# A kernel without the 60 unread one-column products in its order of work

## The chip, the cores and the metric

The kernel runs on one core of a Trainium2 chip. The metric is the time of one execution on the device in microseconds (us). A run is an execution of the whole program; the time before is given as the median of three runs.

## The reference

Two parts follow each other. A recurrent attention (RWKV-7) runs over 768 time steps for 4 batches of 8 heads with a 40 x 40 state, and its output, seen as 3072 tokens of 320 numbers, goes through two dense layers with h * cos(h) between them.

```python
# r, k, v, w, a, b: (4, 8, 768, 40)
for t in range(S):
    kt, vt, rt = (k[:, :, t], v[:, :, t], r[:, :, t])
    wt, at, bt = (w[:, :, t], a[:, :, t], b[:, :, t])
    y[:, :, t] = np.einsum('bhd,bhde->bhe', rt, state)
    Sa = np.einsum('bhde,bhe->bhd', state, at)
    state_decay = state * wt[:, :, None, :] - np.einsum('bhd,bhe->bhde', Sa, bt)
    state = state_decay + np.einsum('bhd,bhe->bhde', vt, kt)
x = y.transpose(0, 2, 1, 3).reshape(3072, 320)
h = x @ w_in               # w_in: (320, 2048)
g = h * np.cos(h)
out = g @ w_out            # w_out: (2048, 320)
```

## The kernel before

The 768 steps are cut into 24 chunks of 32 steps. Within a chunk the recurrence is turned into small matrix products over 32 x 32 and 40 x 72 blocks, one for each batch and head, which TensorE (PE) runs in corners of its array; from chunk to chunk only the state is handed on, in the tile qz. The dense layers then take two chunks at a time, a group of 256 tokens (12 groups), with products of 128 rows and 128, 160 or 256 columns.

The order of all work is written out by hand. The string PLAN is a list of some two thousand tokens, and one loop at the end runs the function of each token (table ACTS); nothing reorders them, so each engine's queue holds its instructions in the order of the tokens. A token is a name and its numbers. Those that matter here:

- of the recurrence, with the chunk's number: g (tile gram), t (sT), q (qps), x (x0ps), s (sps), z (dps, and on DVE, the vector engine, qz and yt), k (kT), pn (nps, for two chunks);
- ij, steps of the inverse of a triangular matrix, on DVE (inv, inv_tmp);
- of the dense layers, with the group's and the block's number: fa and fb (the first layer: tile ph, read by the tile turns and the product gT), m and ms (the second layer: po and p);
- P, the function shifted_, which the change concerns.

PE's tiles stand in eight banks: four, used in turn, for the recurrence (pool ps_a, by the helper at), two for ph, two for po. Nearly all products are recorded by one helper, mm, so that they all bear line L210. A product of 32-bit floats runs as two passes on PE, each a weight load (PEld) and a product; a transpose runs as one.

P:60 stands once in the list, in the middle of the dense layers' group 7, between r:22 (which has no work on PE) and fa:7:3. On PE it follows the products po of m:7:2:0 and comes ahead of the products ph of fa:7:3 and the products dps of z:17.

```python
def shifted_(n):
    ps = at("pad")
    for _ in range(n):
        mm(ps[:1, :1], idle[:, :1], idle[:, :1], True)
```

The tile idle is 128 x 128 zeros in bf16, written at the start; the tile pad is a bank of ps_a that nothing reads. Each of the 60 is a weight load of one column and a product of one column.

Of the kernel before, what the change touches and what calls it, by code (L numbers as in the profile page):

```python
# [90 lines left out]
u:7:0:0 u:7:0:1 m:7:0:0 u:7:0:2 u:7:0:3 lt:21:a ld:23:b pt:r:5:2 z:16 r:23 kn:18 m:7:0:1 t:17 q:17 fa:7:2  # L91
o:6:0 st:r:5:2 st:r:5:1 tk:16 fb:7:2 x:17 xa:20 rf:v:5 u:7:1:0 u:7:1:1 m:7:1:0 u:7:1:2 lt:22:a k:18 y:7:2:0
xa:21 s:17 pn:20 m:7:1:1 lt:22:w xw:22 lt:23:a y:7:2:2 lt:19:r y:7:2:1 m:7:2:0 o:6:1 pt:v:5:0 u:7:1:3 r:22
P:60 fa:7:3 z:17 tb:16 fb:7:3 lt:23:w y:7:3:0 u:7:2:0 tk:17 tb:17 u:7:2:1 u:7:2:2 u:7:2:3 y:7:3:1 y:7:3:2 t:18
g:18 m:7:2:1 m:7:3:0 st:v:5:0 ld:19:k xa:22 xw:23 xa:23 u:7:3:0 u:7:3:1 q:18 pb:22 ld:19:v sp:20 u:7:3:2
m:7:3:1 c:7:0 c:7:1 c:7:3 pt:v:5:1 pn:22 fa:8:0 is:20 ij:20:31 ij:20:30 pt:v:5:2 fb:8:0 x:18 y:8:0:0 ij:20:29
kn:19 u:7:3:3 ms:7 y:8:0:1 y:8:0:2 ij:20:28 s:18 c:7:2 ij:20:27 k:19 ij:20:26 st:v:5:1 ld:20:k lt:21:r
ij:20:25 u:8:0:0 ij:20:24 fa:8:1 u:8:0:1 z:18 ld:20:v fb:8:1 lt:19:v g:19 kn:20 t:19 st:v:5:2 m:8:0:0 ij:20:23
u:8:0:2 ld:21:k ij:20:22 ij:20:21 lt:20:v q:19 y:8:1:0 tk:18 y:8:1:2 ld:21:v k:20 m:8:0:1 y:8:1:1 lt:20:r
ij:20:20 x:19 o:7:0 ij:20:19 m:8:1:0 u:8:1:0 u:8:1:1 u:8:1:2 u:8:0:3 u:8:1:3 ij:20:18 ij:20:17 fa:8:2 ij:20:16  # L100
s:19 fb:8:2 tb:18 z:19 y:8:2:1 m:8:1:1 y:8:2:0 y:8:2:2 o:7:1 tk:19 tb:19 t:20 ij:20:15 ij:20:14 fa:8:3
ij:20:13 ij:20:12 ij:20:11 u:8:2:0 u:8:2:1 q:20 kn:21 fb:8:3 g:20 y:8:3:0 y:8:3:1 k:21 m:8:2:0 u:8:2:2 u:8:2:3
y:8:3:2 ij:20:10 ij:20:9 m:8:2:1 ij:20:8 ij:20:7 ij:20:6 ij:20:5 lt:21:v g:21 u:8:3:0 ij:20:4 ij:20:3 fa:9:0
ij:20:2 ij:20:1 ie:20 m:8:3:0 u:8:3:1 u:8:3:2 u:8:3:3 x:20 fb:9:0 y:9:0:1 m:8:3:1 c:8:0 c:8:1 s:20 lt:22:v
ms:8 c:8:2 ld:22:k y:9:0:0 y:9:0:2 c:8:3 fa:9:1 z:20 ld:22:v kn:22 ld:23:v u:9:0:0 m:9:0:0 u:9:0:1 u:9:0:2
tk:20 t:21 q:21 fb:9:1 y:9:1:1 y:9:1:0 lt:22:r u:9:0:3 y:9:1:2 x:21 m:9:0:1 lt:23:r fa:9:2 s:21 tb:20 fb:9:2
y:9:2:0 z:21 u:9:1:0 u:9:1:1 m:9:1:0 u:9:1:2 u:9:1:3 ld:23:k k:22 t:22 g:22 q:22 m:9:1:1 o:8:0 o:8:1 y:9:2:1
y:9:2:2 u:9:2:0 u:9:2:1 fa:9:3 fb:9:3 x:22 tk:21 m:9:2:0 u:9:2:2 u:9:2:3 y:9:3:0 y:9:3:1 y:9:3:2 lt:23:v kn:23
s:22 m:9:2:1 u:9:3:0 z:22 u:9:3:1 tb:21 fa:10:0 fb:10:0 y:10:0:1 y:10:0:0 m:9:3:0 u:9:3:2 t:23 k:23 m:9:3:1
c:9:0 u:9:3:3 ms:9 y:10:0:2 fa:10:1 c:9:1 q:23 c:9:2 c:9:3 u:10:0:0 fb:10:1 u:10:0:1 m:10:0:0 u:10:0:2  # L110
m:10:0:1 tk:22 u:10:0:3 y:10:1:1 y:10:1:0 y:10:1:2 g:23 o:9:0 fa:10:2 u:10:1:0 u:10:1:1 tb:22 m:10:1:0 o:9:1
u:10:1:2 x:23 fb:10:2 y:10:2:0 y:10:2:1 y:10:2:2 s:23 u:10:1:3 m:10:1:1 u:10:2:0 fa:10:3 u:10:2:1 z:23 tk:23
fb:10:3 y:10:3:1 m:10:2:0 u:10:2:2 m:10:2:1 y:10:3:0 y:10:3:2 m:10:3:0 u:10:3:0 u:10:3:1 u:10:3:2 u:10:2:3
u:10:3:3 tb:23 fa:11:0 fb:11:0 y:11:0:1 y:11:0:0 y:11:0:2 m:10:3:1 c:10:0 ms:10 c:10:1 c:10:3 c:10:2 fa:11:1
fb:11:1 u:11:0:0 u:11:0:1 m:11:0:0 u:11:0:2 o:10:0 y:11:1:0 u:11:0:3 y:11:1:1 m:11:0:1 u:11:1:0 y:11:1:2
u:11:1:1 fa:11:2 fb:11:2 m:11:1:0 u:11:1:2 u:11:1:3 y:11:2:1 y:11:2:0 y:11:2:2 m:11:1:1 fa:11:3 u:11:2:0
u:11:2:1 fb:11:3 y:11:3:0 m:11:2:0 u:11:2:2 m:11:2:1 y:11:3:1 u:11:3:0 y:11:3:2 o:10:1 u:11:3:1 m:11:3:0
u:11:2:3 u:11:3:2 m:11:3:1 c:11:0 c:11:1 u:11:3:3 ms:11 c:11:2 o:11:0 c:11:3 o:11:1
"""

GROUPS = "0+1 2+3 4+5 6+7 8+9 10+11 12+13 14+15 16+17 18+19 20+21 22+23"
# [1109 lines left out]
```

## Time and profile before

| | |
|---|---|
| time, median of 3 runs | 762.61 us (758.38 to 766.61) |
| the profiled execution | 755.39 us, span 753.7 us from the first to the last instruction |
| mean granted clock of PE | 0.983 |
| busy: PE, weight loads (PEld), DVE, ACT, POOL | 702.8, 578.2, 534.8, 398.0, 245.8 us |
| tile pad | 60 products on PE from 541.9 to 543.4 us, 163 ns each, overlapping |
| queue 8, kind "instruction" | 141 packets, 2.31 MB |

PE's products are pipelined, so 60 that take 163 ns each can stand within 1.6 us. A row of the timeline gives the start, how long the merged instructions took, engine, line, operation, tile written <- tiles read, shape, how many, and in brackets how long the engine was idle before and what released it; "issue" there means that the profile shows nothing that it waited for. A row of the windows gives a stretch in us, its length, the busy time and number of instructions of PE, PEld, DVE, ACT and POOL, PE's granted clock, the DMA engines' busy share and GB/s. A piece of the chain of waits gives start, duration and what ran. A DMA queue's row gives packets, MB and the share of the 16 DMA engines' time.

### The profile page before, as it was taken

The numbers are of one execution on the slowest core, as the hardware profiler recorded it, in microseconds if no ns is written. First come the engines' busy times: TensorE is split into PE (matmuls) and PEld (weight loads), VectorE is DVE, ScalarE is ACT, GpSimd is POOL, SyncE is SP. The second block draws the span as 40 slices with busy tenths as digits, with TensorE's granted clock in tenths as the row PEclk, the third lists the DMA queues.
The fourth block names the chain that finished last, engine by engine and source line by source line (L and its number), as shares of the span: only waits on it lengthen the run. The fifth ranks groups of instructions, "written<-read, shape, count | busy, mean of one in ns | idle before, by whom it ended". The sixth has DMA issues, their size and how long they took to land.

```text
span 753.7 us, 40220 instructions
## 1 busy us (share of the span) xinstructions
PE 702.8 (93%) x17956; PEld 578.2 (77%) x17956; DVE 534.8 (71%) x1199; ACT 398.0 (53%) x764; POOL 245.8 (33%) x427
## 2 busy tenths in 40 slices
PE   4659899999999999989999999999999999999995
PEld 2546577777777777878888888888888788888885
DVE  7799888976467777568987758998367984534442
ACT  1335575775656665655645746546456444544442
POOL 8545304221241442450440442332242412321211
PEclk9779999999999999999999999999999999999998
DMA  7667455564565657655656667557543212110000
GB/s 118 130 168 183 149 152 136 116 132 75 117 119 113 123 107 145 130 130 115 139 118 110 128 130 155 107 118 120 102 78 76 62 41 59 48 29 13 21 18 17
DMA packets 267580, 78.11 MB, mean 104 GB/s; under 512 B 229104, under 2 KB 260848, under 8 KB 267408
## 3 DMA queue, kind: packets, MB, share of 16 engines
q1 hardware_dynamic: 264976, 73.66, 46.7%
q8 instruction: 141, 2.31, 1.3%
q0 software_dynamic: 1344, 1.72, 1.2%
q10 hardware_dynamic: 1088, 0.16, 0.1%
q14 instruction: 31, 0.25, 0.1%
HBM read 54.53 MB, written 20.97 MB: 100 GB/s over the span
## 4 chain that ended last, share of the span: by engine, by line
PE 69%; DVE 13%; ACT 5%; DMA 4%; SPq 4%; issue 3%; POOL 1%; DVEq 0%; POOLq 0%; ACTq 0%
PE ph L210 28%; PE po L210 17%; PE dps L210 4%; PE x0ps L210 4%; PE gram L210 3%; PE p L210 3%; SPq L262 2%; PE sps L210 2%; PE qps L210 2%; DVE inv L659 2%; PE nps L210 2%; DVE inv_tmp L655 2%; DVE gT L1010 2%; PE sT L807 1%; DMA nat_v<-in_v_dram 1%
## 5 line engine op out<-in xcount | busy, mean ns | idle before, releaser
L210 PE MATMUL ph<-xT,w_in_sb 128*128 128x256 f32 x768 | 184.3, 386 | 2.5 <-issue 1.0
L210 PEld LDWEIGHTS ph<-xT,w_in_sb 128*128 128x128 f32 x768 | 139.8, 190 | 31.1 <-issue 12.0
L210 PE MATMUL po<-w_out_sb,gT 128*128 128x160 f32 (+1 forms) x624 | 130.3, 347 | 3.0 <-DVE gT L1010 2.3
L1002 DVE SCALAR_TENSOR_TENSOR turns<-turns,ph 128x512 f32<-128x512 f32 x96 | 63.6, 685 | 93.5 <-ACT turns L1000 93.2
L1000 ACT ACTIVATE turns<-ph,few 128x512 f32<-128x512 f32 x96 | 63.6, 686 | 120.2 <-PE ph L210 110.1
L210 PEld LDWEIGHTS po<-w_out_sb,gT 128*128 128x128 f32 x624 | 97.1, 190 | 21.5 <-DVE gT L1010 3.3
L917 POOL TENSOR_TENSOR qz<-qz,wc 128x160 f32<-128x160 f32 x92 | 40.0, 457 | 132.5 <-DVE qz L916 132.5
L1010 DVE TENSOR_TENSOR gT<-ph,turns 128x512 f32<-128x512 f32 x96 | 64.4, 684 | 21.1 <-ACT turns L1007 20.8
L1007 ACT ACTIVATE turns<-turns,few 128x512 f32<-128x512 f32 x96 | 69.3, 722 | 3.1
L1006 ACT ACTIVATE turns<-turns 128x512 f32<-128x512 f32 x96 | 60.1, 626 | 12.4 <-DVE turns L1002 12.3
L1090 POOL TENSOR_TENSOR s<-gT 128x256 f32<-128x256 f32 x36 | 26.9, 747 | 97.3 <-DVE gT L1086 97.3
L210 PE MATMUL ph<-xT,w_in_tail 64*128 64x256 f32 (+1 forms) x464 | 54.5, 396 | 0.0
L291 ACT COPY nat_a<-ws 128x416 f32<-128x416 f32 (+1 forms) x45 | 45.1, 1019 | 16.9 <-DMA wdv<-nat_a 5.7
L210 PE MATMUL po<-TW,gT 128*128 128x160 f32 x288 | 51.4, 300 | 1.8 <-DVE gT L1086 1.2
L659 DVE TENSOR_TENSOR inv<-inv,inv_tmp 128x31 f32<-128x31 f32 (+15 forms) x124 | 50.0, 404 | 4.2
L1082 POOL TENSOR_TENSOR s<-gT 128x256 f32<-128x256 f32 x36 | 27.2, 757 | 78.7 <-DVE gT L1010 72.7
L825 ACT COPY qz<-qps 40x256 f32<-40x256 f32 x92 | 33.8, 367 | 30.8 <-PE qps L210 29.3
L655 DVE TENSOR_TENSOR inv_tmp<-u,inv 128x31 f32<-128x31 f32 (+15 forms) x124 | 46.5, 375 | 2.7
L566 POOL TENSOR_TENSOR bn<-nat_b,rw 128x320 f32<-128x320 f32 x22 | 19.3, 878 | 84.8 <-DVE rw L565 39.2
L210 PEld LDWEIGHTS po<-TW,gT 128*128 128x128 f32 x288 | 42.9, 190 | 2.8 <-DVE gT L1086 1.9
L565 DVE RECIPROCAL rw<-nat_w 128x320 f32<-128x320 f32 x20 | 42.6, 2139 | 0.0
L916 DVE TENSOR_TENSOR qz<-dps,qz 128x160 f32<-128x160 f32 x92 | 29.2, 317 | 16.8 <-PE dps L210 16.8
(158 smaller groups left out, 1248.5 us busy)
## 6 DMA issues: line engine op xcount, KB each, us to landing
words<-in_moe_w_in_dram SPq DMA_DIRECT2D x8, 512.0 KB
xd<-yt SPq DMA_DIRECT2D x48, 80.0 KB
out_dram<-ot SPq DMA_DIRECT2D x24, 160.0 KB
nat_v<-in_v_dram SPq DMA_DIRECT2D x90, 40.0 KB
nat_k<-in_k_dram SPq DMA_DIRECT2D x90, 40.0 KB
nat_b<-in_b_dram SPq DMA_DIRECT2D x84, 40.0 KB
wd<-ws SPq DMA_DIRECT2D x5, 640.0 KB
nat_w<-wd SPq DMA_DIRECT2D x80, 40.0 KB
```

Source lines behind the costliest of these rows:

```text
L210: nc.tensor.matmul(o, lhsT=lhsT, rhs=rhs, start=start, stop=stop, skip_group_check=True)
L291: nc.scalar.copy(quad_part(n, q, i).rearrange("p (d t) -> p d t", t=C), ws[:, :, PARTS[i]].rearrange("p t d -> p d t"))
L565: nc.vector.reciprocal(rw, wn)
L655: nc.vector.tensor_tensor(tmp, u[:, j : j + 1, :j].to_broadcast([P, C - j, j]), x[:, j:, j : j + 1].to_broadcast([P, C - j, j]), ALU.mult,)
L659: nc.vector.tensor_tensor(x[:, j:, :j], x[:, j:, :j], tmp, ALU.subtract)
L825: nc.scalar.copy(pick(qz[rows], f * (NZ - C), (NZ, 2 * B), (1, C)), ps[f][rows, : 2 * B * C].rearrange("p (i t) -> p i t", t=C),)
L917: nc.gpsimd.tensor_tensor(z, z, wc.rearrange("p (b f m) -> p f m b" if re_laid("w", c // 4) else "p (f m b) -> p f m b", f=2, m=2)[:, :, : ...
L1000: nc.scalar.activation(t, u, ACTF.Identity, bias=rnd, scale=1.0)
L1002: nc.vector.scalar_tensor_tensor(t, t, -ROUND, u, ALU.add, ALU.subtract)
L1006: nc.scalar.activation(t, t, ACTF.Abs)
L1007: nc.scalar.activation(t, t, ACTF.Sin, bias=half_pi, scale=-2.0 * math.pi)
L1010: nc.vector.tensor_tensor(gT[:, 2 * e : 2 * e + 2, :n], phs[e], ns[e].rearrange("p (f t) -> p f t", f=2), ALU.mult)
```

## The change

The token P:60 is taken out of PLAN. The lines of the string are filled anew, which changes nothing but where they break; the tokens' order stays. The function shifted_ stays, unused.

```diff
 ... m:7:2:0 o:6:1 pt:v:5:0 u:7:1:3 r:22
-P:60 fa:7:3 z:17 tb:16 fb:7:3 lt:23:w y:7:3:0 u:7:2:0 tk:17 tb:17 u:7:2:1 u:7:2:2 u:7:2:3 y:7:3:1 y:7:3:2 t:18
-g:18 m:7:2:1 m:7:3:0 ...
+fa:7:3 z:17 tb:16 fb:7:3 lt:23:w y:7:3:0 u:7:2:0 tk:17 tb:17 u:7:2:1 u:7:2:2 u:7:2:3 y:7:3:1 y:7:3:2 t:18 g:18
+m:7:2:1 m:7:3:0 ...
```

In the program, PE has 60 weight loads and 60 products fewer at that place; the other engines' queues and SP's DMA queue hold the same instructions in the same order.

More of the change, by code (lines that the diff above doesn't have):

```diff
@@ L93 @@
 xa:21 s:17 pn:20 m:7:1:1 lt:22:w xw:22 lt:23:a y:7:2:2 lt:19:r y:7:2:1 m:7:2:0 o:6:1 pt:v:5:0 u:7:1:3 r:22
-P:60 fa:7:3 z:17 tb:16 fb:7:3 lt:23:w y:7:3:0 u:7:2:0 tk:17 tb:17 u:7:2:1 u:7:2:2 u:7:2:3 y:7:3:1 y:7:3:2 t:18
-g:18 m:7:2:1 m:7:3:0 st:v:5:0 ld:19:k xa:22 xw:23 xa:23 u:7:3:0 u:7:3:1 q:18 pb:22 ld:19:v sp:20 u:7:3:2
-m:7:3:1 c:7:0 c:7:1 c:7:3 pt:v:5:1 pn:22 fa:8:0 is:20 ij:20:31 ij:20:30 pt:v:5:2 fb:8:0 x:18 y:8:0:0 ij:20:29
-kn:19 u:7:3:3 ms:7 y:8:0:1 y:8:0:2 ij:20:28 s:18 c:7:2 ij:20:27 k:19 ij:20:26 st:v:5:1 ld:20:k lt:21:r
@@ L98 @@
[L98 to L117, printed above, removed]
@@ L118 @@
-u:11:2:3 u:11:3:2 m:11:3:1 c:11:0 c:11:1 u:11:3:3 ms:11 c:11:2 o:11:0 c:11:3 o:11:1
+fa:7:3 z:17 tb:16 fb:7:3 lt:23:w y:7:3:0 u:7:2:0 tk:17 tb:17 u:7:2:1 u:7:2:2 u:7:2:3 y:7:3:1 y:7:3:2 t:18 g:18
+m:7:2:1 m:7:3:0 st:v:5:0 ld:19:k xa:22 xw:23 xa:23 u:7:3:0 u:7:3:1 q:18 pb:22 ld:19:v sp:20 u:7:3:2 m:7:3:1
+c:7:0 c:7:1 c:7:3 pt:v:5:1 pn:22 fa:8:0 is:20 ij:20:31 ij:20:30 pt:v:5:2 fb:8:0 x:18 y:8:0:0 ij:20:29 kn:19
+u:7:3:3 ms:7 y:8:0:1 y:8:0:2 ij:20:28 s:18 c:7:2 ij:20:27 k:19 ij:20:26 st:v:5:1 ld:20:k lt:21:r ij:20:25
@@ new lines @@
+u:8:0:0 ij:20:24 fa:8:1 u:8:0:1 z:18 ld:20:v fb:8:1 lt:19:v g:19 kn:20 t:19 st:v:5:2 m:8:0:0 ij:20:23 u:8:0:2
+ld:21:k ij:20:22 ij:20:21 lt:20:v q:19 y:8:1:0 tk:18 y:8:1:2 ld:21:v k:20 m:8:0:1 y:8:1:1 lt:20:r ij:20:20
+x:19 o:7:0 ij:20:19 m:8:1:0 u:8:1:0 u:8:1:1 u:8:1:2 u:8:0:3 u:8:1:3 ij:20:18 ij:20:17 fa:8:2 ij:20:16 s:19
+fb:8:2 tb:18 z:19 y:8:2:1 m:8:1:1 y:8:2:0 y:8:2:2 o:7:1 tk:19 tb:19 t:20 ij:20:15 ij:20:14 fa:8:3 ij:20:13
+ij:20:12 ij:20:11 u:8:2:0 u:8:2:1 q:20 kn:21 fb:8:3 g:20 y:8:3:0 y:8:3:1 k:21 m:8:2:0 u:8:2:2 u:8:2:3 y:8:3:2
@@ new lines @@
+ij:20:10 ij:20:9 m:8:2:1 ij:20:8 ij:20:7 ij:20:6 ij:20:5 lt:21:v g:21 u:8:3:0 ij:20:4 ij:20:3 fa:9:0 ij:20:2
+ij:20:1 ie:20 m:8:3:0 u:8:3:1 u:8:3:2 u:8:3:3 x:20 fb:9:0 y:9:0:1 m:8:3:1 c:8:0 c:8:1 s:20 lt:22:v ms:8 c:8:2
+ld:22:k y:9:0:0 y:9:0:2 c:8:3 fa:9:1 z:20 ld:22:v kn:22 ld:23:v u:9:0:0 m:9:0:0 u:9:0:1 u:9:0:2 tk:20 t:21
+q:21 fb:9:1 y:9:1:1 y:9:1:0 lt:22:r u:9:0:3 y:9:1:2 x:21 m:9:0:1 lt:23:r fa:9:2 s:21 tb:20 fb:9:2 y:9:2:0 z:21
+u:9:1:0 u:9:1:1 m:9:1:0 u:9:1:2 u:9:1:3 ld:23:k k:22 t:22 g:22 q:22 m:9:1:1 o:8:0 o:8:1 y:9:2:1 y:9:2:2
@@ new lines @@
+u:9:2:0 u:9:2:1 fa:9:3 fb:9:3 x:22 tk:21 m:9:2:0 u:9:2:2 u:9:2:3 y:9:3:0 y:9:3:1 y:9:3:2 lt:23:v kn:23 s:22
+m:9:2:1 u:9:3:0 z:22 u:9:3:1 tb:21 fa:10:0 fb:10:0 y:10:0:1 y:10:0:0 m:9:3:0 u:9:3:2 t:23 k:23 m:9:3:1 c:9:0
+u:9:3:3 ms:9 y:10:0:2 fa:10:1 c:9:1 q:23 c:9:2 c:9:3 u:10:0:0 fb:10:1 u:10:0:1 m:10:0:0 u:10:0:2 m:10:0:1
+tk:22 u:10:0:3 y:10:1:1 y:10:1:0 y:10:1:2 g:23 o:9:0 fa:10:2 u:10:1:0 u:10:1:1 tb:22 m:10:1:0 o:9:1 u:10:1:2
+x:23 fb:10:2 y:10:2:0 y:10:2:1 y:10:2:2 s:23 u:10:1:3 m:10:1:1 u:10:2:0 fa:10:3 u:10:2:1 z:23 tk:23 fb:10:3
@@ new lines @@
+y:10:3:1 m:10:2:0 u:10:2:2 m:10:2:1 y:10:3:0 y:10:3:2 m:10:3:0 u:10:3:0 u:10:3:1 u:10:3:2 u:10:2:3 u:10:3:3
+tb:23 fa:11:0 fb:11:0 y:11:0:1 y:11:0:0 y:11:0:2 m:10:3:1 c:10:0 ms:10 c:10:1 c:10:3 c:10:2 fa:11:1 fb:11:1
+u:11:0:0 u:11:0:1 m:11:0:0 u:11:0:2 o:10:0 y:11:1:0 u:11:0:3 y:11:1:1 m:11:0:1 u:11:1:0 y:11:1:2 u:11:1:1
+fa:11:2 fb:11:2 m:11:1:0 u:11:1:2 u:11:1:3 y:11:2:1 y:11:2:0 y:11:2:2 m:11:1:1 fa:11:3 u:11:2:0 u:11:2:1
+fb:11:3 y:11:3:0 m:11:2:0 u:11:2:2 m:11:2:1 y:11:3:1 u:11:3:0 y:11:3:2 o:10:1 u:11:3:1 m:11:3:0 u:11:2:3
@@ L119 @@
+u:11:3:2 m:11:3:1 c:11:0 c:11:1 u:11:3:3 ms:11 c:11:2 o:11:0 c:11:3 o:11:1
 """
```

## The prediction

> **What bounds the kernel now.** I read the first part of the page, then the windows by stage, then the chain of waits.
>
> ```profile
> span 753.7 us, 40220 instructions
> PE 702.8 (93%) x17956; PEld 578.2 (77%) x17956; DVE 534.8 (71%) x1199; ACT 398.0 (53%) x764; POOL 245.8 (33%) x427
> ```
> ```profile
> 541.90:600.00 58.10, 57.58 (x1661) 49.70 (x1664) 40.09 (x105) 29.24 (x59) 21.28 (x35) 1.00 0.32 67
> 600.00:650.00 50.00, 49.32 (x1387) 42.47 (x1380) 34.00 (x90) 25.67 (x54) 12.96 (x21) 1.00 0.23 54
> 650.00:700.00 50.00, 49.71 (x1080) 42.47 (x1079) 21.55 (x52) 21.25 (x41) 11.57 (x17) 1.00 0.08 21
> ```
> TensorE (PE, first column of busy time) sets the end: behind the 60 products, from 541.9 to 700 us, it is idle for 1.5 us of 158, and its clock is granted in full (1.00). What is taken from PE there, or put in its way, reaches the end nearly whole. The 60 products stand at 541.9:
>
> ```profile
> 537.88 2.37 PE po L210 x16
> 540.26 0.50 issue
> 540.75 1.25 PE po L210 x8
> 542.00 1.57 PE pad L210 x60
> 543.57 1.92 PE ph L210 x8
> ```
> The chain of waits ran through them: PE goes from po to pad to ph without a pause, so they hide in no wait. The 0.50 us of "issue" just ahead is the other thing to see: PE stands still, and nothing in the profile releases it. The timeline of PE's weight loads shows that stop and some more of them:
>
> ```profile
> 332.88 0.24 PEld L210 LDWEIGHTS gram<-rT,vp 40*32 40x32 f32 x31 [0.96 <-issue]
> ...
> 448.81 0.30 PEld L210 LDWEIGHTS ph<-xT,w_in_sb 128*128 128x128 f32 x2 [1.39 <-issue]
> ...
> 470.94 0.49 PEld L210 LDWEIGHTS gram<-rT,vp 40*32 40x32 f32 x46 [0.44 <-issue]
> ...
> 540.76 0.46 PEld L210 LDWEIGHTS po<-w_out_sb,gT 128*128 128x128 f32 x3 [0.61 <-issue]
> ```
> They fall in the middle of a run of like products, where nothing is waited for. I counted PE's queue in program order (weight loads, products and waits on semaphores; an f32 product is two passes, a load and a product each, a transpose is one): these four stand at places 16578, 22722, 23746 and 27330. Divided by 256, each leaves 194. Between 300 and 541.9 us PE stops for over 0.2 us at nine places with that remainder, 5.5 us in all; behind the 60 products it stops at none. The DMA view of that later stretch says what comes every 256 instructions:
>
> ```profile
> q8 instruction: 32, 0.52, 1.3%
> ```
> This is queue 8 from 541.9 to 700 us: 32 packets of 16 KB, in the time in which the windows count 4128 products and 4123 loads, so one for about 256 instructions. These are PE's own instructions on their way in. Before the stop at 540.76 the packet began at 538.34 and took 0.93 us, and PE went on 1.49 us after its end; the next one began at 541.89, 1.13 us after PE had gone on. So PE holds the block that it is in and the next; when it steps into a block it sends for the one after. From that step to use: 1.05 us until the packet starts (0.8 to 1.2 at 23 of the 34 edges behind the 60 products), 0.95 us for the packet (0.88 to 1.36 there), 1.45 us until PE can use it (1.37 to 1.58 at the nine stops): **3.45 us, an estimate from these rows**. PE stops where it runs 256 instructions in less. On average a block takes 4.9 us, but 128 small gram products are 256 instructions in some 1.3 us. Behind the 60 products as they now stand, the block edges fall so that the shortest block takes 3.43 us (580.40 to 583.83), and it just passes.
>
> **The change, part by part.** Removed: 60 products and 60 weight loads on PE and the tile pad; no row waits for pad. On the other engines and on SP's queue no instruction is added, removed or moved.
>
> (1) The products themselves. From 541.93, the first pad, to 543.50, the first ph, is 1.57 us, on the path. The ph products behind need nothing later than what po had, so all of it goes: **-1.57 us**. Bounds: 0, if PE then waits for something else, and -1.57.
>
> (2) The bank of pad. Four banks go round; pad took one, and the four dps tiles of z:17 follow at once and take all four, with or without it. Nothing is late for it: 0.
>
> (3) All that PE does behind place 27346 stands 120 instructions earlier. In the old count the block edges move by 120, to remainder 314 - 256 = 58. I laid the new edges over the old timeline and asked of each block how long PE takes from entering it to needing the next (PE reads a run of instructions some 8 ahead, as its semaphore instructions show, but not past a wait: 10 places behind the wait for kT that ended at 229.16 it sent for a block at 229.35). Against 3.45 us:
>
> - 608.05 (gram) to 610.11 (ph): 2.06 us, so a stop of **1.4**.
> - 645.9 (gram, just after its wait for kT) to 647.21 (qps): 1.3 us, a stop of **2.1**. This block holds 227 instructions of gram and 29 of qps.
> - 685.30 (po) to 688.12 (x0ps): 2.82 us, a stop of **0.6**; the block ahead of it, entered at 682.0 in gram, is **0.15** late, which takes away the lead that po would have had.
> - 622.2 (ph) to 625.59 (dps), **0.1**; 632.35 (x0ps) to 635.68 (ph), **0.1**; 654.5 (x0ps) to 657.85 (sps) and on to 661.13 (dps), **0.15 each**.
> - 581.1 to 584.63, across po and x0ps: 3.5 us, **0**. PE had read ahead: a semaphore instruction 13 places behind the edge ran at 581.13.
>
> The rest have 0.2 us or more to spare. The rows of the two dearest places:
>
> ```profile
> 608.05 0.76 PE L210 MATMUL gram<-aT,kT 40*32 40x32 f32 x64
> 608.68 0.75 PE L210 MATMUL gram<-rT,vp 40*32 40x32 f32 x64
> 609.36 1.99 PE L210 MATMUL ph<-xT,w_in_sb 128*128 128x256 f32 x8
> ```
> ```profile
> 645.84 0.72 PE L210 MATMUL gram<-aT,kT 40*32 40x32 f32 x62
> ...
> 647.06 0.81 PE L210 MATMUL qps<-rT,s 40*40 40x32 f32 x64
> 647.80 0.81 PE L210 MATMUL po<-TW,s 128*128 128x160 f32 x4
> ```
> The sum of the stops is 1.4 + 2.1 + 0.6 + 0.15 + 0.1 + 0.1 + 0.15 + 0.15 = **4.75 us**. From below: with 3.3 us for a fetch and PE reading 32 instructions ahead, it is 3.2; from above, with 3.6 us and no lead, 8.4. I take 4.75, because at 3.45 us the same sum over the old edges gives 0 stops behind the 60 products, as the trace has it. What is late next is what follows on PE itself; DVE, ACT and POOL are fed by PE and move with it. Only from 594 to 607 does the chain run through DVE (the inv steps), and no stop is foreseen there.
>
> Together: -1.57 + 4.75 = **+3.2 us**. The profiled execution (755.39 us, span 753.7) would be 758.6; it was faster than all three timed runs, so I add the 3.2 to their median: 762.61 + 3.2 = **765.8 us**.
>
> [...]
>
> **The rivals.**
>
> A. The fetches stay hidden and the products were pure cost: 762.61 - 1.57 = 761.0 us. For it: behind 541.9 us the trace shows no stop, and most DMA traffic is over (share 0.32, then 0.23 and 0.08, against 0.62 to 0.64 from 200 to 541.9). Against it: the gram run at 645.9 asks for a block after 1.3 us, and no packet in the trace took less than 0.87 us, before the 1.05 and the 1.45.
>
> B. The other side: the fetch is slower than 3.45 us where SP's transfers are in flight, and every block under 4 us pays. Its place is 541.9 to 600, with new blocks of 3.7 to 3.8 us at 555.98, 565.72 and 569.43, and 3.3 us blocks later on. For it: in the busier stretch before, a packet began up to 4.4 us after PE entered the block (384.11, entered at 379.66). With a median delay of 0.5 us more, ten places pay 0.5 each on top of the above: +3.2 + 5 = +8.2, 770.8 us. It decides from a fetch of about 3.9 us on. Against it: behind 541.9 us only two packets started more than 1.35 us after the edge, and none 1.7.
>
> C. Without the 60 products PE waits elsewhere, and the 1.57 us come back as idle time: +4.75, 767.4 us. For it: at 585 the chain passes through ACT and DVE (qz, turns, gT). Against it: that work is itself started by PE's qps at 580.33, which would come earlier too.
>
> **How the numbers follow.** Forecast 0.58, A 0.20, B 0.15, C 0.07. The forecast's own terms reach from -1.57 + 3.2 = +1.6 to -1.57 + 8.4 = +6.8, so 764.2 to 769.4. A lies at 761.0, B at 770.8; and a median of few runs moves (the three lie between 758.38 and 766.61), so the range is widened by a little over 1 us on each side: 759.5 to 772.0. 1% is 7.6 us, about what a measurement of this kernel can tell from no change. Forecast, A and C lie within it; B lies just beyond. Faster by over 1% 0.03, for the spread of medians alone; slower 0.17; same 0.80.
>
> **What would show each step.** The pad rows gone, and the ph behind them straight after po. New stops by "issue" in the middle of the gram or ph rows at about 607 to 612 and of the qps rows near 647 (shifted by the time so far), the latter over 1.5 us; remainder 194 again in the new count; queue 8 with 140 or 141 packets. PE's busy time down by about 1.6, its idle time behind 541 up by 4 to 6. Wrong would be: a span shorter by 1.5 (A: no stops at the places named), stops before 600 us (B), or a new wait of PE for DVE or ACT of over 1 us between 543 and 600 (C).

## The result, and the profile after

The kernel without the 60 products takes 767.66 us, median of 20 runs (762.28 to 772.8), against 761.55 us, median of 20 runs of the kernel before (756.38 to 766.61). The ratio is 1.0085, 95% interval [1.0065, 1.0105]: about 6 us slower, with less work to do. (The ratios here and below are not the quotients of the medians, and leave out two slow executions.) The profiled execution took 764.57 us, its span is 762.8 us and PE's mean granted clock 0.976; before it was 755.39, 753.7 and 0.983.

First the head of the page after. PE has 60 products and 60 weight loads fewer, and yet it is busy for 5.6 us longer (702.8 before); the instruction queue is as it was.

```profile
span 762.8 us, 40100 instructions
PE 708.4 (93%) x17896; PEld 582.0 (76%) x17896; DVE 536.2 (70%) x1199; ACT 399.0 (52%) x764; POOL 245.6 (32%) x427
...
q8 instruction: 141, 2.31, 1.3%
```

The windows by stage, as shown of before (start and end, length, then busy time and count of PE, PEld, DVE, ACT, POOL, then PE's granted clock, DMA share, GB/s). PE's idle time from 541.9 to 700 us is 58.10 - 56.27 + 50.00 - 48.34 + 50.00 - 47.04 = 6.45 us, where it had been 1.5. And the column that was 1.00 in all three rows is 0.97 in two of them:

```profile
541.90:600.00 58.10, 56.27 (x1526) 48.62 (x1526) 38.02 (x102) 28.75 (x57) 19.15 (x32) 0.97 0.32 65
600.00:650.00 50.00, 48.34 (x1313) 41.04 (x1312) 33.99 (x86) 24.31 (x50) 13.93 (x22) 1.00 0.22 51
650.00:700.00 50.00, 47.04 (x1026) 40.79 (x1018) 20.34 (x49) 19.23 (x40) 11.45 (x17) 0.97 0.10 27
```

The chain of waits after (start, duration, what ran). The pad piece of 1.57 us is gone, and ph follows po at once. Further on "issue" stands at five dear places, in the middle of runs of like products:

```profile
541.33 0.50 issue
541.83 1.25 PE po L210 x8
543.08 1.73 PE ph L210 x8
...
577.34 1.22 issue
578.56 0.36 PE gram L210 x25
578.91 1.24 PE sT L807 x8
580.15 2.94 PE po L210 x12
...
587.63 0.37 issue
...
613.06 0.99 issue
614.04 1.24 PE ph L210 x5
...
650.83 0.28 PE qps L210 x14
651.11 2.16 issue
653.28 0.69 PE qps L210 x47
653.96 3.12 PE po L210 x12
...
669.15 0.52 issue
```

These stops stand at places in PE's program that leave 194 when divided by 256, in the new count (the three dearest at 29378, 31170 and 33218): the block edges moved by 120 instructions, as foretold. With 0.28 at 696.95 and pieces of 0.19 and 0.05 these stops come to 5.8 us.

The second thing to see lies in the rows behind two of the stops. The 12 products po took 2.94 and 3.12 us; the same pieces took 1.65 and 1.83 in the kernel before, whose chain ran through these places without a pause:

```profile
576.54 1.28 PE gram L210 x87
577.83 0.85 PE sT L807 x8
578.68 1.65 PE po L210 x12
...
647.13 0.74 PE qps L210 x64
647.87 1.83 PE po L210 x12
```

Windows of 2 us in the trace of after show why. The granted clock there is half:

```profile
580.00:582.00 2.00, 2.00 (x9) 2.00 (x9) 1.44 (x5) 0.56 (x2) 0.00 (x0) 0.50 0.26 40
...
654.00:656.00 2.00, 2.00 (x9) 2.00 (x10) 0.16 (x1) 1.46 (x4) 0.73 (x1) 0.58 0.33 87
```

The trace's clock records give two periods of 3.41 us at half clock between 541 and 760 us (from 579.2 and from 654.3) and one ahead of them (333.5); before, there is none between 60 and 749 us. Each costs about 1.7 us, half of its length. At 579 the rows that it stretched give 1.68: sT 1.24 for 0.85 and po 2.94 for 1.65. At 654 it is po, 3.12 for 1.83, and the ph behind it.

From the first ph product of fa:7:3, where the pads have just been passed, to the end, the trace counts 219.87 us, and 210.18 before: +9.69. Less the 1.57 us of the pads that is +8.1. The other 1.0 us of the 9.1 by which the spans differ arises ahead of that place, where both programs are the same.

### The profile page after: what moved, and what is told of

Read it like the earlier page. It is cut to its first block, busy times and chain, and to the rows that moved or that the text cites. A ratio compares the mean times of both kernels' runs of the same rounds, so it can differ in the third digit from the quotient of the medians.

```text
span 762.8 us, 40100 instructions
## 1 busy us (share of the span) xinstructions
PE 708.4 (93%) x17896; PEld 582.0 (76%) x17896; DVE 536.2 (70%) x1199; ACT 399.0 (52%) x764; POOL 245.6 (32%) x427
## 4 chain that ended last, share of the span: by engine, by line
PE 74%; DVE 12%; issue 4%; SPq 4%; ACT 3%; DMA 2%; POOL 0%; DVEq 0%; ACTq 0%; POOLq 0%
PE ph L210 27%; PE po L210 18%; PE dps L210 5%; PE x0ps L210 4%; PE gram L210 3%; SPq L262 3%; PE p L210 3%; PE sps L210 2%; PE qps L210 2%; DVE inv_tmp L655 2%; DVE inv L659 2%; PE busy L210 2%; PE nps L210 2%; PE sT L807 2%; DVE gT L1010 2%
## 5 line engine op out<-in xcount | busy, mean ns | idle before, releaser
L210 PE MATMUL po<-w_out_sb,gT 128*128 128x160 f32 (+1 forms) x624 | 132.4, 351 | 2.5 <-DVE gT L1010 1.8
L210 PEld LDWEIGHTS po<-w_out_sb,gT 128*128 128x128 f32 x624 | 99.2, 193 | 20.7 <-DVE gT L1010 2.7
L210 PEld LDWEIGHTS ph<-xT,w_in_tail 64*128 64x128 f32 (+1 forms) x464 | 32.6, 168 | 11.2 <-issue 6.0
```

Of the source, the lines that this page charges most:

```text
L210: nc.tensor.matmul(o, lhsT=lhsT, rhs=rhs, start=start, stop=stop, skip_group_check=True)
```

## The experiments

The theory: PE's instruction blocks end at other places now, and PE runs some blocks faster than the next arrives; that, and a clock that falls behind a long stop, is the loss. The rival: the pads were good in themselves, as a pause or as a filler at that place. All times are medians; each ratio is against runs of the kernel before on the same chip (762.65 us for the first four, 761.53 for the next two, 758.86 for the last two).

### More pads, with the edges of the one and of the other kernel

128 pads are 256 instructions, so behind them every block edge is where it is with none. 188 pads put the edges where 60 put them.

```diff
-P:60 fa:7:3 z:17
+P:128 fa:7:3 z:17
```


> 128 products in place of the 60, at the same place: 256 PE instructions, so every block edge behind them falls on the same instructions as without any. Theory F (what counts is where the 256-instruction edges fall): the stops of the kernel without products come back at the same tiles (gram, ph, qps, dps, x0ps, about 6 us), and the products themselves cost 128 x 26 ns = 3.35 us, so 767.7 + 3.3 = 771.0 us, +9.4 against before. Theory P (idle products at 541 us do something useful where they stand: they keep PE in step or its clock up): no slower than before by more than their extra 1.8 us, 763.4.

```diff
-P:60 fa:7:3 z:17
+P:188 fa:7:3 z:17
```


> 188 products at the same place: 376 PE instructions, 120 more than a full block, so the edges fall as with 60. Theory F: no stop behind them, and 128 products more than before at 26 ns: 761.6 + 3.3 = 764.9 us. It has 60 idle products more than p128 and should be about 6 us faster than it. Theory P or any other in which products cost or help by their number: slower than p128 by 60 x 26 ns = 1.6 us, or faster in both.

Measured: 128 pads 776.08 us, ratio 1.0188 [1.0146, 1.023]; 188 pads 767.17 us, ratio 1.0068 [1.0035, 1.01]. Sixty products more, and 8.9 us faster, where the expectation was about 6. The chain of waits with 128 has the stops of the changed kernel, in the same runs of products:

```profile
588.82 1.46 issue
590.28 0.35 PE gram L210 x26
...
624.62 0.93 issue
...
662.77 2.14 issue
```

With 188 the qps run, all 64 in one piece, has none, as before:

```profile
658.00 0.74 PE qps L210 x64
```

The edges decide, not the pads: both have more pads than the kernel before, and the dear stops come back in one and not in the other. The times of both are above what was expected, by 5 and by 2 us, of which 1 us is the chip's (762.65 us for the kernel before, where 761.6 was reckoned with). The windows of the 188 show a further reason: at 550 the clock fell to half, though PE counts as busy all of the time, with pads. The eight ph products behind them took 3.71 us, where they took 1.92 before.

```profile
550.00:554.00 4.00, 4.00 (x84) 3.60 (x80) 0.00 (x0) 0.00 (x0) 0.00 (x0) 0.55 0.01 4
```

From the first ph behind the pads to the end this trace is 2.5 us longer than that of before, and 2.4 of it arises in the first 6 us, at half clock.

### The 60 pads at other places

```diff
-P:60 fa:7:3 z:17
+fa:7:3 z:17
...
+P:60 t:10
```


> The 60 products moved ahead of t:10, at about 300 us. Behind 541 us all edges fall as before; between 300 and 541 us they fall 120 instructions off. Theory F: the same model of blocks (3.5 to 3.9 us for a fetch) that gives 2 to 7 us of stops for the edges of before gives 13 to 20 us for these, so 10 to 14 us slower than before, 771 to 776 us, with the new stops all between 300 and 541 us, and the stops at 332.9, 448.8, 470.9 and 540.8 gone or elsewhere. Theory P: if the products serve at 541 us, it is as slow as without them (767.7) with the stops behind 541; if only their number counts, it is equal to before, 761.6.

```diff
-P:60 fa:7:3 z:17
+fa:7:3 z:17
...
-ld:23:k k:22
+ld:23:k P:60 k:22
```


> The 60 products moved ahead of k:22, at about 647 us. Theory F: up to there the run is that of the kernel without products (stops near 559, 573, 577, 588 and 613 us, about 2.8 us, and 1.5 us lost to a window of half clock), behind it that of before (no stop of 2.2 us in qps, none in dps and x0ps): 761.6 + 2.8 + 1.5 = 765.9 us, some 2 us faster than without products. Theory P: with the products away from 541 us, the same as without them plus their time, 769.2.

Measured: ahead of t:10, which the trace has at 338.5 us and not near 300, 776.95 us, ratio 1.0204 [1.0159, 1.0249], a little above the 771 to 776 that were expected; ahead of k:22, near 650 us, 766.72 us, ratio 1.0055 [1.0025, 1.0084]. In the early one the edges between the two places have moved, and the new stops are there. The dearest, in the chain of waits:

```profile
454.42 3.15 issue
457.58 0.73 PE qps L210 x54
```

From 430 to 560 us its chain has 8.5 us of issue in pieces of 0.2 us or more (2.6 before over the same work), and the clock falls to half four times (342.4, 458.5, 516.5, 557.5). From the first ph of fa:7:3 to its end it takes 211.12 us, 0.9 more than before, all of that within its first 27 us, where PE waits 0.89 us for GpSimd (587.03) and not for a block: the edges are the old ones again and cost nothing. The late one is the mirror of this. Its stops stand ahead of the pads (the first row), and behind them the run that stopped for 2.16 us goes through:

```profile
562.53 2.22 issue
...
650.64 1.57 PE pad L210 x60
...
654.93 0.74 PE qps L210 x64
```

The pads themselves cost 1.57 us here too, so this term is shown at two places. The late one came out near the expected 765.9 us, but its profile is put together otherwise, so the agreement is in part luck. Its stops ahead of the pads should have been those of the changed kernel, and the 1.22 in gram is missing while 2.22 stand in nps at 562.5, where the changed kernel lost 0.19. The packet for that block began 3.57 us after its edge here, and 1.13 in the changed kernel. The period at half clock that was expected did not come: behind 100 us its clock is full up to the last 4 us.

### No pads, but other work in the fast block

The block of the dearest stop holds little but small gram and qps products. Here the large products po of m:9:1:1 come ahead of q:22 in place of behind it.

```diff
-t:22 g:22 q:22 m:9:1:1 o:8:0
+t:22 g:22 m:9:1:1 q:22 o:8:0
```
(without P:60 as well)

> No idle products, and m:9:1:1 (12 large products, 24 instructions, 1.6 us) put ahead of q:22 instead of behind it: nothing but that order changes. Theory F: the block entered in gram at about 650 us then holds 227 instructions of gram, the 24 of po and 5 of qps, so PE runs 1.6 us longer before it needs the next block: the stop of 2.2 us in qps shrinks to 0.5 to 0.7, and the window of half clock behind it goes (1.5 us more). 2 to 3 us faster than without products, ratio to before about 1.005, or 765 us; the stops before 650 us stay. Theory P (the products at 541 us matter where they stand): no change, 767.7, ratio 1.0085.

Measured: 763.6 us, ratio 1.0024 [0.9997, 1.0051]. The block now takes 1.83 us longer to run, and the stop fell by 2.16 - 0.55 = 1.6 us. The one in gram at 581 is untouched:

```profile
581.25 1.23 issue
...
652.62 1.83 PE po L210 x12
654.44 0.19 PE qps L210 x2
654.63 0.55 issue
655.18 0.81 PE qps L210 x59
```

The same work, in the same number of instructions, at the same edges: 4 us less than the changed kernel, 1.6 of it the stop. Against the first profile of the changed kernel, the clock explains more: here it is 1.00 from 541.9 to 700 us. The last of these windows:

```profile
650.00:700.00 50.00, 49.39 (x1142) 42.31 (x1141) 21.03 (x51) 21.69 (x44) 13.22 (x20) 1.00 0.11 30
```

That the clock held behind the stop in gram too, which is as long as in the changed kernel, is not the exchange's doing. From the first ph of fa:7:3 to the end this trace takes 215.02 us, 4.8 less than the first profile of the changed kernel, but only 0.1 less than the second one (215.11, shown further down), in which the clock held as well. A stop of 1.04 us in nps at 562.28, whose packet began 2.81 us after its edge, took back most of what the exchange saved. So the shorter stop in qps is shown to come from the exchange; the rest of the 4 us is not.

### A stop without a block edge

Is it the standing still that halves the clock, or the late block? Here the kernel before gets a stop of another kind at that place: two of the 60 pads stand between g:22 and q:22, and the second reads a tile that passes through DVE and 20 copies on GpSimd (POOL). Between the two places the edges lie four instructions further on, behind them they are the old ones.

```diff
-P:60 fa:7:3
+P:58 fa:7:3
...
-g:22 q:22
+g:22 Q:18 q:22
```


> The kernel before with 58 products instead of 60, and between g:22 and q:22 two one-column products, the second of which waits for a chain over DVE and GpSimd (20 small copies) that the first one sets off: PE stands still for some 3 to 4 us at about 647 us, with the block edges behind it as before (60 products in all). It leaves nothing of the computation out. Theory C (PE standing still for more than some 1.8 us of a 3.41 us window halves the clock granted in the next window): a window of 0.5 right behind the stop, no other such window between 100 and 740 us, and the large products there take 1.7 times as long, so the cost is the stop plus about 1.5 us, 766 to 767 us. Rival (the half clock came with the late instruction blocks, not with the standing still): clock 1.0 behind the stop, and the cost is the stop alone, 765 us.

Measured: 771.94 us (4 runs), ratio 1.0142 [1.011, 1.0174]. The stop was twice as long as meant, 6.87 us, and its rows in the timeline and in the windows are:

```profile
660.89 0.16 PE L210 MATMUL pad<-idle,gate 128*1 128x1 bf16 x1 [6.87 <-POOL gate L1194]
660.99 1.29 PE L210 MATMUL qps<-rT,s 40*40 40x32 f32 x64
662.21 1.43 PE L210 MATMUL po<-TW,s 128*128 128x160 f32 x4
```
```profile
657.50:660.90 3.40, 0.01 (x1) 0.01 (x1) 0.00 (x0) 0.00 (x0) 2.66 (x13) 0.50 0.04 11
660.90:664.30 3.40, 3.40 (x73) 3.32 (x74) 0.00 (x0) 1.47 (x4) 0.52 (x1) 0.50 0.02 5
```

The clock is half from 657.5 us, in the second half of the stop, and for the period after the stop; qps takes 1.29 where it took 0.81, po 1.43 where it took 0.81. From the first ph of fa:7:3 the trace is 8.8 us longer than before: 6.87 stop, 0.1 the two pads, 1.8 the clock. No block was late. Standing still was enough here, where it filled a whole period (654 to 657.5 us, with PE busy for 0.02 of 3.5 us). One point of the expectation failed: there is another stretch at half clock, from 121.6 to 128.4 us, long before the stop, behind a period in which PE stood still for 1.42 us.

### The changed kernel again, and a second exchange

The changed kernel once more, without an edit:

> The changed kernel once more, on one chip with the next one. Theory: the stops stand at the same instructions (dps, gram, qps) and are 5 to 6 us behind 541 in sum; if the packet for the block that begins in dps near 573 starts some 3 us after the step again, the stop in gram near 578 is 1.2 to 1.7 again, which would make it a property of the place. 1.006 to 1.010 of the kernel before. Rival: the late packet of the first profile was a single one, the stop in gram is gone, and the time is nearer 1.005.

and the exchange above with m:8:0:0 moved ahead of g:19 besides, into the block that gram runs through at 577:

```diff
-g:19 kn:20 t:19 st:v:5:2 m:8:0:0 ij:20:23
+m:8:0:0 g:19 kn:20 t:19 st:v:5:2 ij:20:23
```


> The order of the experiment without the 60 products and with m:9:1:1 ahead of q:22, and besides m:8:0:0 (large products po) ahead of g:19 in place of behind t:19, so that the large products stand in the block that the gram products run through too fast near 578. Theory: the stop of 1.2 us in gram goes or falls under 0.5, the granted clock stays 1.00 from 541 to 700, and the time falls below the 1.0024 of the order with one move, to 0.999 to 1.002 of the kernel before. Rival: the packet is late whatever runs in the block, and the stop moves to the large products or to the tile behind them; then about 1.0025. Second rival: gram and sT come later and the recurrence (DVE and ACT behind qps) makes PE wait near 585; then 1.003 to 1.006 with a wait of PE for DVE or ACT.

Measured: the changed kernel 766.0 us (8 runs), ratio 1.0087 [1.0058, 1.0115]; the two exchanges 761.88 us, ratio 1.002 [0.9987, 1.0053].

The second profile of the changed kernel separates the two costs. The dear stops are at the same instructions (besides the two shown, 0.38 in ph and 0.28 in dps), and the windows behind the dearest one have the full clock:

```profile
581.13 1.19 issue
582.31 0.36 PE gram L210 x26
...
652.66 2.00 issue
654.67 0.68 PE qps L210 x47
```
```profile
654.00:656.00 2.00, 1.33 (x55) 1.29 (x55) 1.10 (x2) 0.59 (x2) 0.00 (x0) 1.00 0.34 97
```

From the first ph of fa:7:3 to the end it took 215.11 us: 4.93 more than before, against 9.69 in the first profile. Laid over each other, the two traces part by 1.7 us at each of the two periods at half clock, 3.4 of the 4.8 us; the rest is longer stops. Its span of 762.1 us is nearly that of the first all the same: 5.1 us arose ahead of the pads' place, in work that is the same in all these kernels but the one with the early pads. It ends between 541.9 and 550.0 us in these nine executions, without an order by the number of pads. That is why whole spans of two profiles can't be set against each other here, and stretches can.

Why did the clock hold this time? Its records come in periods of 3.41 us (in the first profile 72 of them from 333.5 to 579.2 and 22 from there to 654.3), and their phase differs from run to run (by 0.9 us between the profile of before and the first of the changed kernel). In the first profile the stop of 2.16 us fell whole into one of them, and the next ran at half. In the second an end of a period (653.3) cut the stop into 0.60 and 1.40, and nothing happened. Over all ten profiles of this case (behind 100 us and ahead of the last 25, periods with pads aside), a period in which PE stood still for 1.85 us or more was followed by half clock all six times; one with 0.94 to 1.7 us 6 times of some 35; one with less only once (0.18 us, the first period of the stretch at 121.6 us above, itself at half clock). So a period idle for about half of its length was enough each time, and one idle for a third sometimes.

With the two exchanges both large stops are gone (qps 0.22, none in gram), but the block from which the po products were taken became fast in turn:

```profile
583.64 1.58 PE x0ps L210 x103
585.22 1.23 issue
586.45 0.32 PE x0ps L210 x5
```

The stop moved, as its first rival had it, though not for that rival's reason. That gram doesn't stop is no proof for the second exchange: the packet for that block came 1.12 us after its edge this time, not 3 (more on this below), and would have been in time anyway. At 761.88 us this order is 4 us faster than the changed kernel on the same chip, and not measurably other than the kernel before: no version here is measurably faster than that.

## Why the prediction was right, and where it was not

The forecast was +3.2 us, within 1% and slower; measured are +6.1 us and +0.85%. Step by step:

(1) The products. -1.57 us, as foretold; they hid in no wait, and the pads cost the same 1.57 at 650 us.

(2) The bank. No row behind the pads waits for one. Nothing speaks against 0.

(3) The block edges. The mechanism is shown: same edges, same stops (128 pads); old edges, no such stops in the chain (188); the stops go with the place of the pads (early, late), and fall when the block takes longer (exchange). The sum, 4.75 us, was 5.8 us of issue in the first profile and 4.0 in the second; by distances it is 4.93 in the second. But the parts are less good than the sum. Foretold 2.1 in qps: 2.16 and 2.00. Foretold 1.4 in ph: 0.99 and 0.38, since PE had read further ahead (in the second profile the packet began 0.17 us behind the edge before it, not 1.05). Foretold 0.6 in x0ps: 0.28 and none. Foretold 0.15 in dps: 0.52 and 0.28. The x0ps at 587, foretold 0, lost 0.37 in the first profile. In the second a wait for ACT and DVE (turns, gT) covered it; the chain of before ran through these engines from 581.1 to 585.4 us too, which the sentence that only 594 to 607 runs through DVE overlooks. And the step that says the rest have 0.2 us or more to spare was wrong at two places: gram at 577, foretold nothing, stopped for 1.22 and 1.19 us, and nps at 559 for 0.19 in the first profile.

In gram the term of 1.05 us from edge to packet was the one mis-sized. Its median is about 1.0 in both profiles of the changed kernel, but at the edge in dps at 573.0 the packet began 3.29 us late, at the same instruction 3.07 in the second profile, 3.03 with 128 pads and 3.30 in the first exchange; with the pads at 650 us and with two exchanges it was 1.01 and 1.12, and gram didn't stop, although the program up to that edge is the same in these. So four of six executions had it late, and neither the place alone nor a rare accident explains that. The edge before nps shows the same: 1.13 and 1.09 us in the two profiles of the changed kernel, 2.81 and 3.57 in the first exchange and with the late pads. What holds the packet back is open. The DMA engines were idle from 574 to 576 us (share 0.00), so it isn't traffic, and rival B's mechanism, fetches made slow by SP's transfers, isn't what the traces show; its stops before 600 us were there all the same.

What the prediction lacked is the clock. A stop was counted at its own length, and each long one can cost some 1.7 us more behind it. Behind 541 us that came to 3.4 us in the first profile and to nothing in the second: the change is +8.1 us in the first, and +3.4 (4.93 - 1.57) in the second. One of its signs failed by the clock: PE's busy time was to fall by 1.6 us and rose by 5.6 (ahead of the last 14 us the clock records of after have ten periods at half clock, those of before six; 4 x 1.7 = 6.8 us). The median of +6.1 lies between. For a mean cost I can only estimate: on the chip of the second profile the runs of the changed kernel have a mean clock of 0.9759 and take 765.7 us (8 runs), those of before 0.9778 and 759.8 us (19 runs). A period of 3.41 us at half clock lowers the mean by 3.41 x 0.5 / 762 = 0.0022, so 0.0019 is nearly one period more, some 1.5 us. This is rough, for the clocks of the eight runs alone lie between 0.972 and 0.981. With the +3.4 of the second profile that makes 4.9 of 5.9 us; the last 1.0 is within the interval of the ratio (4.4 to 8.7 us), and not explained.

Rival A (the fetches stay hidden) is refuted by the stops in the chains above. In the first profile of the changed kernel 8 of the 30 edges from 543 to 700 us show such a stop: four where PE came to the next edge 1.5 to 3.1 us after the one before, and four where the packet began late (3.3 and 1.65 us after its edge) or took long (1.58 and 1.46 us); at the other 22 the fetch was hidden. Rival C (the 1.57 us come back as a wait for another engine) wasn't seen: in the timeline of after, PE has three idle times between 543 and 600 us, 0.19, 1.22 and 0.37 us, and issue ends all of them.

Rightly read were the remainder of 194, the count of 256 per block (with two passes to a product of 32-bit floats and one to a transpose: the 32 + 32 products of a token g stand as 64 + 64 rows of gram, the 8 transposes of sT as 8), two blocks held (the dearest stop ended at 653.28, 1.48 us after the end of the packet that began 0.97 us behind the edge before it), and the places of the dearest stops. The upper part of the range stood there for slower fetches; it was the clock that filled it. That the time of 767.66 us lies within the range, and even within the 764.2 to 769.4 of the forecast's own terms, is in so far luck: those bounds knew nothing of the clock.

## What to carry to other kernels

Taking the dead instructions out of this long straight program shifted all block edges behind them, here by 120 instructions, so ask, before believing a gain, how long PE takes over each 256 instructions in the new count: a run of small products at the wrong place of a block can cost more than the instructions did (2.16 us in qps, against 1.57 for the pads). What helped here is to put slow products into the fast block, or, as in the kernel before, to pad so that the edges fall well; then look at all blocks again, since the stop can move to the next. Count a stop of about 1 us or more with the half clock that may follow it (about 1.7 us here), and compare stretches of two profiles from a common instruction on, not whole spans.

## What the runs showed of the hardware that was not expected

- In the ten profiles PE's clock fell to half for the next period of 3.41 us after a period in which PE stood still for 1.85 us or more (six of six), and now and then after 0.94 to 1.7 us (6 of some 35). The price was about 1.7 us of PE's work, 1.8 after the stop of 6.87.
- One-column products did not always hold that clock: in 188 of them, 4.77 us without a pause, it fell to half, and behind 128 of them and behind the 60 near 340 us too (554.3, 342.4), though PE counts as busy for all of the 3.40 us ahead of each. Behind the 60 at 541.9 and at 650.6 it held.
- The delay from an edge to its packet was about 1.05 us, but at two places of the program it was 3.8 to 5.1 us in run after run: at the edge in po near 326 us 3.80 to 4.84 in all ten profiles, and at the one in ph near 380 us 4.42 to 5.05 in all nine that have an edge there.
